# A kernel's transform stage: half of one product moves from VectorE to ScalarE and GpSimd

## The chip, the cores and the metric

One core of a Trainium2 chip runs the whole program. The metric is the device time of one execution in microseconds; the kernel before has a median of 1918.08 us over three runs. The engines are PE (TensorE, matrix products), DVE (VectorE), ACT (ScalarE), POOL (GpSimd) and SP (SyncE, which here only issues DMAs). Each engine works through its own queue in order.

## The reference

Two independent parts are computed and put side by side. Part A is a recurrent attention over 64 segments of 32 rows. Part B, which the change touches, is a long convolution done in the frequency domain:

```python
P = jnp.exp(logdA[:, :, None] * l[None, None, :])
K = jnp.einsum('dn,dnl,dn->dl', Cc, P, dB).real
...
Yf = Uf * Kf[None, :, :, :]
y = irfft2(Yf, s=(1, L2), axes=(-2, -1)).astype(jnp.bfloat16)[:, :, 0, :L]
y = (lambda x, *d: x.transpose(*d))(y, 0, 2, 1) + u * Dskip[None, None, :]
```

Here `u` is 2048 x 1024 in bfloat16, `Uf` and `Kf` are the spectra of `u` and of the convolution's kernel, and their complex product is what the stage below computes.

## The kernel before

The program runs part B first and part A after it; the weights that A keeps on the chip are loaded while B works. Part B builds its tables for some 400 us and writes the spectrum of `u` to DRAM (`Ud`). Then comes the stage of this case, the loop `for b in range(16)` (L1542), where `b` stands for a pair of 256 channels (`b // 4`) and a quarter of the frequencies (`b % 4`).

For every `b` there are two classes of frequencies, 0 and 1. For each class PE computes the kernel's spectrum into PSUM (`spectrum`, L1221, 20 matmuls, tile `pa`, two banks: one for each half `h` of the frequencies, each with a real and an imaginary part of 256 channels). The spectrum of `u` for a class is one 512 KB load into `uq[class]` (`load_u`, L1214, tile `wq`). There is one `uq` for each class, so the load for b+1 waits until block b has read it.

DVE then does the complex product, all in float32:

- `times_u` (L1384) makes two products of 1024 elements for a class: Z, the imaginary part of `u` times the kernel's spectrum, into the SBUF tile `Zs` (tile `z`), and X, the real part times it, in place in PSUM. I call them Z0, X0 for class 0 and Z1, X1 for class 1.
- `rotate` (L1389) joins X and Z in two instructions of 512 elements. For class 0 it writes the tile `even` (`y`); this is the first rotation. For class 1 it works in place in PSUM; this is the second rotation.
- sum and difference of the two classes follow (L1483 into `odd`, L1484 into `even`), two instructions of 1024 elements.

POOL then makes four additions of 512 elements for block b (L1486 twice, L1488, L1489), which leave the product's spectrum in bfloat16 tiles (`Bt`). I call them the additions of b. After them POOL multiplies a tile of `u` with `Dskip` (`skips`, L1503). The inverse transform of block b-4 runs on PE beside this, in two parts (`inverses`, 16 matmuls each and one with the identity, L1537), and ACT brings each part out of PSUM (L1538).

The generator `pointwise` (L1461) holds DVE's part and stops once in its middle: before the stop Z0, X0, the first rotation (for b > 3 after the next two), Z1, X1; behind it the second rotation, `odd`, `even` and POOL's additions. The loop body runs the first half, issues spectrum and inverse for PE, and then runs the second half. For b < 3 the second half is run between the two spectra; for b of 3 and more behind both. `now` holds the PSUM tiles for the next block. Three such tiles are used in turn, so the class 1 spectrum of b+1 goes into the tile that class 0 of block b leaves, which is free once the first rotation of b has read it.

Program order decides who waits for whom: an instruction that reads a place waits for the last one ahead of it in the program that wrote it, whatever the engines. `Zs` has one place for each class.

Of the kernel before, what the change touches and what calls it, by code (L numbers as in the profile page):

```python
# [14 lines left out]
ALU = mybir.AluOpType  # L15
# [697 lines left out]
def part_b(ctx, tc, u, A_re, A_im, B_re, B_im, C_re, C_im, log_dt, Dskip, out_b, ahead, copies, residents, first_state):  # L713
# [5 lines left out]
    DH, DQ = 512, 256  # L719
    v, sc, gp, pe, sy = nc.vector, nc.scalar, nc.gpsimd, nc.tensor, nc.sync  # L720
# [57 lines left out]
    with tc.tile_pool(name="b_par", bufs=1) as par, tc.tile_pool(name="b_parh", bufs=2) as parh, \  # L778
# [127 lines left out]
        parts = {}  # L906
# [62 lines left out]
        for word_ in PAR:  # L969
            word = word_.rstrip("/")  # L970
            nm, n_ = word[0], word[1:]
# [234 lines left out]
    def weighted(kc, n_, amp):  # L1206
        a_ = amp.rearrange("p (j q) -> p j q", j=3)[:, :, 256 * n_:256 * n_ + 256]
        g_ = G[kc][:, n_, 2:5].rearrange("p j s h f -> p j s (h f)")
        v.tensor_tensor(out=g_, in0=g_, in1=a_.unsqueeze(2).to_broadcast([128, 3, 2, 256]), op=ALU.mult)
# [4 lines left out]
    def load_u(b, ns=(0, 1), eng=sy):  # L1214
        for n_ in ns:
            eng.dma_start(out=uq[n_], in_=Ud[b % 4, b // 4][:, 2 * n_:2 * n_ + 2].rearrange("p a c d -> p (a c d)"))

    def load_inverse(i):
        sy.dma_start(out=MI[i][:], in_=MId[2 * i:2 * i + 2].rearrange("c p a k q -> p c a k q"))

    def spectrum(b, n_, outs, woven=()):  # L1221
        dq, kc = b // 4, b % 4
        KT = ks[dq // 2]
        d = slice(DQ * (dq % 2), DQ * (dq % 2) + DQ)
        for i in range(20):
            half, cs, j = i // 10, i // 5 % 2, i % 5
            pe.matmul(outs[half][:, cs, :], lhsT=G[kc][:, n_, j, cs, half, :], rhs=KT[j][:, d], start=(j == 0), stop=(j == 4), skip_group_check=True)
            for k in woven[i * len(woven) // 20:(i + 1) * len(woven) // 20]:
                make(k, 1)
# [100 lines left out]
    for f in range(16):  # L1330
# [7 lines left out]
        if f == 15:  # L1338
# [7 lines left out]
            uq = [t_[:].bitcast(F32) for t_ in wsl[1:3]]  # L1346
# [29 lines left out]
    def make(kc, n):  # L1376
        for _ in range(n):
            next(made[kc])

    def halves(pool=ps_e):  # L1380
        t_ = pool.tile([128, 2, 512], F32, name="pa", tag="pa")
        return [t_[:].rearrange("p h (c d) -> p h c d", c=2)]

    def times_u(s_, Z, n_, X=None):  # L1384
        us = uq[n_].rearrange("p (a c d) -> p a c d", a=2, c=2)
        for i, t_ in ((1, Z), (0, s_[n_][0] if X is None else X)):
            v.tensor_tensor(out=t_, in0=us[:, :, i, :].unsqueeze(2).to_broadcast([128, 2, 2, DQ]), in1=s_[n_][0], op=ALU.mult)  # L1387

    def rotate(Y, X, Z):  # L1389
        v.tensor_tensor(out=Y[:, :, 0, :], in0=X[:, :, 0, :], in1=Z[:, :, 1, :], op=ALU.subtract)  # L1390
        v.tensor_tensor(out=Y[:, :, 1, :], in0=X[:, :, 1, :], in1=Z[:, :, 0, :], op=ALU.add)
    now = [halves() for _ in range(2)]
# [56 lines left out]
    Zs, even = (pw.tile([128, *dims], F32, name=nm) for nm, dims in (("z", (2, 2, 2, DQ)), ("y", (2, 2, DQ))))  # L1449

    def blocks(t_):
        return t_.rearrange("p i c d -> p (i c) d")
# [4 lines left out]
    def spectra(dq, kc, odd_):  # L1457
        at = PLACES[dq].split()[2 * kc + odd_]
        return Bp[:, stay_.index(at)] if at in stay_ else Bq[:, ("e2", "o1", "o3", "s2").index(at)]

    def pointwise(b, s_):  # L1461
        dq, kc = b // 4, b % 4
        if b:
            times_u(s_, Zs[:, 0], 0)
            if b < 4:
                rotate(even, s_[0][0], Zs[:, 0])
                if b < 3:
                    weighted(b + 1, 0, amps[b + 1])
                load_u(b + 1, (0,))
                for i in {1: (0,), 2: (4,), 3: ()}[b]:  # L1470
                    load_inverse(i)
                if b == 1:
                    next(resident)
            times_u(s_, Zs[:, 1], 1)
            if b < 15:
                load_u(b + 1, (1,) if b < 4 else (0, 1))
            if b > 3:
                rotate(even, s_[0][0], Zs[:, 0])
        yield
        if b:  # L1480
            rotate(s_[1][0], s_[1][0], Zs[:, 1])
        Y = (even[:], s_[1][0]) if b else (first[:, 0], first[:, 1])
        v.tensor_tensor(out=odd[:], in0=Y[0], in1=Y[1], op=ALU.subtract)  # L1483
        v.tensor_tensor(out=even[:], in0=Y[0], in1=Y[1], op=ALU.add)  # L1484
        for i, op in ((0, ALU.add), (1, ALU.subtract)):
            gp.tensor_tensor(out=spectra(dq, kc, 0)[:, i], in0=even[:, 0], in1=even[:, 1], op=op)  # L1486
        eng, to = v if b == 15 else gp, blocks(spectra(dq, kc, 1))
        eng.tensor_tensor(out=to[:, 0:4:3], in0=odd[:, 0], in1=odd[:, 1, ::-1], op=ALU.add)  # L1488
        eng.tensor_tensor(out=to[:, 2:0:-1], in0=odd[:, 0], in1=odd[:, 1, ::-1], op=ALU.subtract)  # L1489
# [3 lines left out]
    def rows_of(t_, n_):  # L1493
        return t_[CLASSES[n_ % 4]][:, :, DQ * (n_ // 4):DQ * (n_ // 4) + DQ]

    def load_pair(n_, pool, bufs=4):
        uu = held[n_] = pool.tile([128, 2, 2, DQ], BF16, name="uu", tag="uu", bufs=bufs)
        sy.dma_start(out=uu[:].rearrange("p i a d -> p (i a) d"), in_=rows_of(u_v, n_))
# [6 lines left out]
    def inverses(n_, i):  # L1505
        while ended:
            ended.pop(0)()
        inverse(n_ // 4, PAIRS[2 * n_ % 8 + i], held[n_][:, i])
        if i:
            ended.append(lambda: sc.dma_start(out=rows_of(out_v, n_), in_=held[n_][:].rearrange("p i a d -> p (i a) d")))  # L1510
# [30 lines left out]
    w4 = k1[0:4, 3072:4096]  # L1541
    for b in range(16):  # L1542
        points = pointwise(b, now)
        next(points)
        for _ in range(4 if b in (2, 3) else 0):
            second.pop(0)()
        if b == 2:
            ks.append([])
        if 2 <= b < 6:
            lo, hi = b - 2, min(b - 1, 3) if b < 5 else 5  # L1550
            ks[1].extend(load_k(1, k1[:, DH * lo:DH * hi], lo))
        if b >= 4:
            load_pair(b - 2, iv)
        if b == 3:
            v.tensor_scalar(out=ident[:], in0=ident[:], scalar1=float(PLEN / 2), scalar2=None, op0=ALU.mult)
            load_pair(0, iv)
            load_pair(1, iv)
            state = first_state(g0[0:8, 5120:6144], iv.tile([128, 8, 24], BF16, name="xt0", bufs=1))
            next(state)
            ctx_k.close()  # L1560
            ps_h = ctx.enter_context(tc.tile_pool(name="b_psh", bufs=1, space=PSUM))
            ps_y = ctx.enter_context(tc.tile_pool(name="b_psy", bufs=2, space=PSUM))
        if b == 0:
            now = nxt_
        elif b + 1 < 16:
            now = []
            for n_ in range(2):
                if b < 3 and n_:
                    next(points, None)
                    weighted(b + 1, 1, amps[b + 1])  # L1570
                now.append(halves(ps_h if b > 2 and (2 * b + n_) % 3 == 0 else ps_e))
                spectrum(b + 1, n_, [now[n_][0][:, half] for half in range(2)], (3,) * 7 if b == 1 else ())
                if b >= 4:
                    inverses(b - 4, n_)
        next(points, None)
        for n_ in (0, 1) if b == 3 else (b - 2,) if 3 < b < 15 else ():
            skips(n_, gp)
        for i in {1: (1,), 3: (5,), 4: (2, 3), 5: (6, 7)}.get(b, ()):
            load_inverse(i)
        if b == 2:  # L1580
            rows4 = g0[0:4, 5120:6144]
            for half in range(2):
                sy.dma_start(out=rows4[:, DH * half:DH * half + DH], in_=Kx[half][31, NF - 1].rearrange("g c -> (g c)").partition_broadcast(4))
            sy.dma_start(out=w4, in_=u[0:4, :])
            gp.tensor_tensor(out=w4, in0=rows4[:, 0:D], in1=w4, op=ALU.mult)
            gp.memset(l4, 0.0)
            gp.memset(l4[:, :, 127:128], float(PLEN / 2))
            gp.affine_select(out=l4[:, :, 127:128], in_=l4[:, :, 127:128], compare_op=ALU.is_ge, fill=0.0, base=0, pattern=[[1, 4], [0, 1]],
                             channel_multiplier=-1)
        for _ in range({1: 2, 2: 2, 3: 1, 4: 1, 5: 1, 6: 2, 7: 2, 8: 2, 9: 2, 11: 3, 12: 3, 13: 2, 14: 3, 15: 3}.get(b, 0)):  # L1590
            next(resident)
        if b == 10:
            state.send(ps_y.tile([128, 8, 128], BF16, name="yp", tag="yp")[:, :, 0:8])
# [180 lines left out]
```

## Time and profile before

| what | value |
|---|---|
| times of three runs | 1917.59, 1918.08, 1934.71 us |
| profiled execution | 1915.11 us, span of its instructions 1913.4 us |
| transform loop, about 403 to 560 us | 157 us |
| of it blocks 5 to 14, one after the other | 9.65 us for each |
| end of the last inverse, begin of part A | about 577 us |
| part A, from about 592 us on | 1321 us, DMA share 0.93 |

Rows of the timeline give start, length, engine, line, operation, output and input, shape and count; a bracket at the end tells how long the engine had been idle before it and what ended that. Rows of the windows table give, for a stretch of time, its length, then the busy time of PE, PEld (weight loads), DVE, ACT and POOL, the granted TensorE clock (1.00 is full speed), the share of the DMA engines and GB/s. Rows of the chain of waits give start, length and what the chain ran through.

### The profile page before, as it was taken

How to read it: one execution, taken by the hardware profiler on the slowest of the kernel's cores; microseconds unless marked ns; L12 is line 12 of the kernel's file. 1: busy time of each engine (PE TensorE's matmuls, PEld its weight loads, DVE VectorE, ACT ScalarE, POOL GpSimd, SP SyncE). 2: the span in 40 equal slices, each digit the busy share in tenths (PEclk: the TensorE clock that was granted, in tenths of full speed). 3: DMA queues.
4: the chain of work that ended last, by engine and by line, in shares of the span. 5: the costliest groups of instructions: out<-in, count | busy, mean ns of one | idle time of the engine just before them, and what ended most of it. 6: DMA issues, size and time to landing. Idle time of an engine off the chain costs nothing.

```text
span 1913.4 us, 73735 instructions
## 1 busy us (share of the span) xinstructions
PE 1768.3 (92%) x31563; PEld 1088.4 (57%) x31563; DVE 1349.7 (71%) x3367; ACT 921.2 (48%) x1655; POOL 514.4 (27%) x900
## 2 busy tenths in 40 slices
PE   8999999868986989999999999999999999999989
PEld 3666665546773555555555555555555555555554
DVE  8599999899973666666666666766666666666650
ACT  8799999860112434444343444444343444444420
POOL 2354544427770111111111111111111111212120
PEclk9999999898998999999999999999999999999999
DMA  7889898778799999999999999999999999999993
GB/s 220 238 236 266 258 276 249 219 220 293 258 306 357 348 322 342 341 345 337 344 353 344 338 350 351 336 355 343 340 348 354 330 345 346 346 340 347 352 335 95
DMA packets 341744, 594.21 MB, mean 311 GB/s; under 512 B 94100, under 2 KB 216476, under 8 KB 339368
## 3 DMA queue, kind: packets, MB, share of 16 engines
q1 hardware_dynamic: 297944, 534.99, 81.8%
q10 hardware_dynamic: 36816, 29.59, 4.8%
q0 software_dynamic: 6656, 24.92, 3.5%
q8 instruction: 247, 4.05, 0.8%
q14 instruction: 81, 0.66, 0.1%
HBM read 531.92 MB, written 71.63 MB: 315 GB/s over the span
## 4 chain that ended last, share of the span: by engine, by line
PE 46%; DMA 31%; DVE 12%; ACT 5%; issue 3%; POOL 2%; SPq 1%; DVEq 0%; POOLq 0%; ACTq 0%
PE acc L414 22%; DMA wst<-WD_v 11%; DMA wst<-WD_o 9%; PE pp L527 9%; DMA wst<-WD_q 3%; PE pe L667 3%; DMA wst<-WD_k 2%; PE tr L425 2%; PE pro L184 2%; DVE nr L1274 1%; PE pro L197 1%; DMA arena<-PKd 1%; PE pv L495 1%; DMA wq<-Ud 1%; DVE pa L1387 1%
## 5 line engine op out<-in xcount | busy, mean ns | idle before, releaser
L414 PEld LDWEIGHTS <-a_hT 128*32 128x32 bf16 x12351 | 329.6, 96 | 327.3 <-issue 76.1
L420 ACT CAST arena<-acc 128x512 bf16<-128x512 f32 x384 | 225.2, 586 | 395.1 <-PE acc L414 326.8
L414 PE MATMUL acc<-wst,a_hT 128*32 128x512 bf16 x2308 | 230.1, 382 | 35.3 <-DMA wst<-WD_v 26.1
L527 PEld LDWEIGHTS <-arena 128*32 128x32 bf16 x8256 | 215.4, 96 | 76.9 <-issue 53.6
L428 POOL COPY arena<-arena 128x128 bf16<-128x128 bf16 x128 | 37.6, 294 | 697.6 <-PE tr L425 364.9
L335 DVE TENSOR_SCALAR arena<-keep 128x256 int32<-128x256 int32 x508 | 174.3, 395 | 27.9 <-PE acc L414 27.9
L414 PE MATMUL acc<-XM,a_hT 128*32 128x512 bf16 x2560 | 184.2, 380 | 0.0
L414 PE MATMUL acc<-W,a_hT 128*32 128x512 bf16 x1536 | 132.8, 384 | 0.0
L197 PE MATMUL pro<-XM,wsl 128*128 128x512 bf16 x512 | 124.6, 387 | 2.6 <-DVE kst L206 1.5
L454 DVE TENSOR_REDUCE a_mx<-sc 128x4 f32<-128x160 f32 (+1 forms) x192 | 71.8, 374 | 74.2 <-PE sc L442 72.9
L527 PE MATMUL pp<-W_o,arena 128*32 128x256 bf16 x3584 | 121.7, 273 | 2.3 <-issue 2.2
L544 DVE COPY arena<-tr 128x512 bf16<-128x512 bf16 x64 | 27.2, 425 | 126.3 <-PE tr L425 126.3
L458 ACT ACTIVATE sc<-sc 128x160 f32<-128x160 f32 (+1 forms) x192 | 63.9, 333 | 106.5 <-DVE sc L455 106.0
L462 DVE TENSOR_REDUCE a_mx<-sc 128x4 f32<-128x160 f32 (+1 forms) x192 | 72.7, 379 | 55.2 <-ACT sc L458 54.9
L489 POOL TENSOR_TENSOR arena<-arena,a_BD 128x128 bf16<-128x128 bf16 x128 | 51.3, 401 | 211.5 <-DVE arena L472 201.3
L414 PE MATMUL acc<-W_q,a_hT 128*32 128x512 bf16 x1536 | 107.9, 379 | 0.0
L1274 DVE TENSOR_SCALAR nr<-ptt 128x456 f32<-128x456 int16 x128 | 80.3, 628 | 31.3 <-PE ptt L1252 28.3
L1266 ACT ACTIVATE E<-pa 128x648 bf16<-128x648 f32 x128 | 87.7, 712 | 16.9 <-PE pa L1258 15.2
L623 ACT CAST arena<-pp 128x128 bf16<-128x128 f32 x64 | 17.0, 266 | 154.8 <-DVE arena L623 154.8
L527 PE MATMUL pp<-wst,arena 128*32 128x256 bf16 x1536 | 76.4, 274 | 16.4 <-DMA wst<-WD_o 15.0
L513 ACT CAST arena<-pv 128x512 bf16<-128x512 f32 (+1 forms) x128 | 61.4, 479 | 59.6 <-PE pv L499 33.4
L425 PEld LDWEIGHTS <-arena 128*128 128x128 bf16 x1024 | 57.6, 98 | 54.8 <-issue 25.9
(334 smaller groups left out, 3967.7 us busy)
## 6 DMA issues: line engine op xcount, KB each, us to landing
wst<-WD_v SPq DMA_DIRECT2D x256, 512.0 KB
wst<-WD_k SPq DMA_DIRECT2D x192, 512.0 KB
wst<-WD_o SPq DMA_DIRECT2D x192, 512.0 KB
wst<-WD_q SPq DMA_DIRECT2D x128, 512.0 KB
Ud<-ux POOLq DMA_DIRECT2D x16, 1024.0 KB, 7.5
wq<-Ud SPq DMA_DIRECT2D x32, 512.0 KB
wsl<-in_A_Wk_dram SPq DMA_DIRECT2D x16, 512.0 KB
wsl<-in_A_Wv_dram SPq DMA_DIRECT2D x16, 512.0 KB
```

Of the source, the lines that this page charges most:

```text
L197: nc.tensor.matmul(a[:], lhsT=w[:, kc, 128 * j:128 * j + 128], rhs=xTl[:, kc, :, :].rearrange("p s k -> p (s k)"), start=(kc == 0), stop=( ...
L335: nc.vector.tensor_scalar(out=out.bitcast(I32), in0=in_.bitcast(I32), scalar1=0, scalar2=None, op0=ALU.bitwise_or)
L414: nc.tensor.matmul(a[32 * g:32 * g + 32, o_:o_ + rhs.shape[1]], lhsT=hT[:, kc, :], rhs=rhs, start=(kc == 0), stop=(kc == KC - 1), tile_pos ...
L420: nc.scalar.copy(out=q, in_=a[:])
L425: nc.tensor.transpose(out=p[:, hl, :, :].rearrange("p a b -> p (a b)"), in_=q[:, 128 * hl:128 * hl + 128], identity=ident[:])
L454: nc.vector.tensor_reduce(out=m_, in_=x, axis=AX.X, op=ALU.max)
L458: nc.scalar.activation(out=flat(sc, i), in_=flat(sc, i), func=ACT.Exp, scale=scale)
L462: nc.vector.tensor_reduce(out=m_, in_=x, axis=AX.X, op=ALU.add)
L513: copy(out=o[:, i:i + n], in_=p[:, i:i + n, :].rearrange("p a (g q) -> p a g q", g=4))
L527: nc.tensor.matmul(po[32 * qt:32 * qt + 32, o_:o_ + rhs.shape[1]], lhsT=oT[:, h % 4, (h % 16) // 4, :], rhs=rhs, start=False, stop=(h == 3 ...
L1266: sc.activation(out=T["E", r, e // 4][:, lo:lo + 8 * NE].rearrange("p (i c) -> p i c", i=2), in_=T.pop(("p", r, e))[:, :, 0:4 * NE], func= ...
L1274: v.tensor_scalar(out=T["n", r, e // 4][:, lo:lo + 8 * NT], in0=T.pop(("t", r, e))[:, 0:8 * NT].bitcast(I16)[:, 0:16 * NT:2], scalar1=floa ...
```

## The change

For class 1 DVE's Z1 now covers only the first half of the frequencies (512 elements instead of 1024). For the second half, ACT copies the kernel's spectrum from PSUM into the place in `Zs` (`moved`), and POOL multiplies it there with the imaginary part of `u` (`shared`). The rest of the product is as it was.

```diff
-    def times_u(s_, Z, n_, X=None):
+    def times_u(s_, Z, n_, X=None, parts=2):
         us = uq[n_].rearrange("p (a c d) -> p a c d", a=2, c=2)
-        for i, t_ in ((1, Z), (0, s_[n_][0] if X is None else X)):
-            v.tensor_tensor(out=t_, in0=us[:, :, i, :]..., in1=s_[n_][0], op=ALU.mult)
+        for i, m, t_ in ((1, parts, Z), (0, 2, s_[n_][0] if X is None else X)):
+            v.tensor_tensor(out=t_[:, 0:m], in0=us[:, 0:m, i, :]..., in1=s_[n_][0][:, 0:m], op=ALU.mult)
+    def moved(s_):
+        sc.copy(out=Zs[:, 1, 1], in_=s_[1][0][:, 1])
+    def shared():
+        us = uq[1].rearrange("p (a c d) -> p a c d", a=2, c=2)
+        gp.tensor_tensor(out=Zs[:, 1, 1], in0=us[:, 1, 1, :]..., in1=Zs[:, 1, 1], op=ALU.mult)
...
             times_u(s_, Zs[:, 0], 0)
+            if b > 3 and b < 15:
+                load_u(b + 1, (0,))
...
-            times_u(s_, Zs[:, 1], 1)
+            times_u(s_, Zs[:, 1], 1, parts=1)
             if b < 15:
-                load_u(b + 1, (1,) if b < 4 else (0, 1))
+                load_u(b + 1, (1,))
...
         if b == 0:
             now = nxt_
+            moved(now)
+            shared()
         elif b + 1 < 16:
...
                 spectrum(b + 1, n_, ...)
+                if n_ and b + 1 >= 1:
+                    moved(now)
                 if b >= 4:
                     inverses(b - 4, n_)
+        if b > 2 and b < 15:
+            shared()
         next(points, None)
+        if 0 < b < 3 and b + 1 >= 1:
+            shared()
```

The copy for block b+1 is issued behind the class 1 spectrum of b+1, in the body of block b. The POOL product for b+1 comes after the second half of `pointwise` of b for b = 1 and 2, and ahead of it for b = 0 and for b from 3 to 14. The two loads of `uq` for b+1 were issued together behind X1 for b > 3; now the first stands behind X0.

More of the change, by code (lines that the diff above doesn't have):

```diff
@@ L1382, in halves @@
         return [t_[:].rearrange("p h (c d) -> p h c d", c=2)]
-    def times_u(s_, Z, n_, X=None):
+    def times_u(s_, Z, n_, X=None, parts=2):
         us = uq[n_].rearrange("p (a c d) -> p a c d", a=2, c=2)
-        for i, t_ in ((1, Z), (0, s_[n_][0] if X is None else X)):
-            v.tensor_tensor(out=t_, in0=us[:, :, i, :].unsqueeze(2).to_broadcast([128, 2, 2, DQ]), in1=s_[n_][0], op=ALU.mult)
+        for i, m, t_ in ((1, parts, Z), (0, 2, s_[n_][0] if X is None else X)):
+            v.tensor_tensor(out=t_[:, 0:m], in0=us[:, 0:m, i, :].unsqueeze(2).to_broadcast([128, m, 2, DQ]), in1=s_[n_][0][:, 0:m], op=ALU.mult)
+    def moved(s_):
+        sc.copy(out=Zs[:, 1, 1], in_=s_[1][0][:, 1])
+    def shared():
+        us = uq[1].rearrange("p (a c d) -> p a c d", a=2, c=2)
+        gp.tensor_tensor(out=Zs[:, 1, 1], in0=us[:, 1, 1, :].unsqueeze(1).to_broadcast([128, 2, DQ]), in1=Zs[:, 1, 1], op=ALU.mult)
     def rotate(Y, X, Z):
```

## The prediction

> **What bounds the kernel now.** I read the page first, then the windows table over the transform loop, then the timeline of one block, and the chain of waits for the loads of u.
>
> ```profile
> PE 1768.3 (92%) x31563; PEld 1088.4 (57%) x31563; DVE 1349.7 (71%) x3367; ACT 921.2 (48%) x1655; POOL 514.4 (27%) x900
> ```
>
> ```profile
> 453.00:560.00 107.00, 99.28 (x850) 81.64 (x849) 104.83 (x112) 13.85 (x24) 77.69 (x57) 0.99 0.90 296
> ```
>
> Over the whole span PE is the busiest. In the blocks from b = 5 on it is DVE, with 104.83 of 107 us; ACT has 93 us free there and POOL 29. One block, b = 8, shows how they hang together:
>
> ```profile
> 481.08 1.22 DVE L1484 TENSOR_TENSOR y<-y,pa 128x1024 f32<-128x1024 f32 x1
> 482.22 1.22 DVE L1387 TENSOR_TENSOR z<-wq,pa 128x1024 f32<-128x1024 f32 x1
> ...
> 482.38 2.50 POOL L1486 TENSOR_TENSOR Bt<-y 128x512 bf16<-128x512 f32 x2 [2.53 <-DVE y L1484]
> ...
> 482.89 2.35 PE L1227 MATMUL pa<-k,XM 128*128 128x256 bf16 x20
> ...
> 483.35 1.22 DVE L1387 TENSOR_TENSOR pa<-wq,pa 128x1024 f32<-128x1024 f32 x1
> ...
> 484.48 1.22 DVE L1387 TENSOR_TENSOR z<-wq,pa 128x1024 f32<-128x1024 f32 x1
> 484.60 2.59 SPq L1216 DMA_DIRECT2D wq<-Ud  x2
> ...
> 485.08 1.91 PE L1525 MATMUL yp<-Bt,MI 128*128 128x256 bf16 x16
> 485.62 1.22 DVE L1387 TENSOR_TENSOR pa<-wq,pa 128x1024 f32<-128x1024 f32 x1
> ...
> 486.75 0.68 DVE L1390 TENSOR_TENSOR y<-pa,z 128x512 f32<-128x512 f32 x1
> 486.82 0.38 PE L1537 MATMUL yp<-uu,b_ident 128*128 128x512 bf16 x1
> ...
> 487.29 0.60 ACT L1538 ACTIVATE uu<-yp 128x512 bf16<-128x512 f32 x1 [3.60 <-PE yp L1537]
> 487.30 2.13 POOL L1503 TENSOR_TENSOR uu<-uu,Dsk 128x1024 bf16<-128x1024 bf16 x1
> 487.35 0.68 DVE L1391 TENSOR_TENSOR y<-pa,z 128x512 f32<-128x512 f32 x1
> ...
> 487.94 0.69 DVE L1390 TENSOR_TENSOR pa<-pa,z 128x512 f32<-128x512 f32 x1
> ...
> 488.08 2.34 PE L1227 MATMUL pa<-k,XM 128*128 128x256 bf16 x20 [0.88 <-DVE y L1391]
> ...
> 490.73 1.22 DVE L1484 TENSOR_TENSOR y<-y,pa 128x1024 f32<-128x1024 f32 x1
> ...
> 491.87 1.21 DVE L1387 TENSOR_TENSOR z<-wq,pa 128x1024 f32<-128x1024 f32 x1
> ```
>
> The block lasts from Z0 to the next Z0: 491.87 - 482.22 = 9.65 us, and DVE has no gap in it. The class 1 spectrum of b+1 starts at 488.08, 0.05 us after the first rotation of b ends (487.35 + 0.68): PE waits for DVE. In the program the second rotation (487.94) needs nothing but DVE's own work.
>
> **What the change takes away.** Z1 loses half. Instructions of 1024 elements follow each other at 1.13 us (484.48, 485.62), those of 512 at 0.60 (486.75, 487.35), so DVE saves 0.53 us in each block, 15 blocks, 8 us if nothing else came of it.
>
> **What it moves without effect.** The two loads of u look as if the first had waited behind X1. But the pair begins at 484.60, just as X0 ends (483.35 + 1.22 = 484.57), and ends at 487.19, with X1's end at 486.84 between: SP held each one until its own product had read the tile. To issue the first behind X0 in the program changes nothing: 0 us. The uu load and the weight loads behind it on SP keep their places.
>
> **What it adds.** The copy is 512 float32 from PSUM on ACT; the nearest row is L1538 at 0.60 us with the same input. The POOL product has two float32 inputs and a float32 output of 512; the row with that shape:
>
> ```profile
> L1016 POOL TENSOR_TENSOR ux<-us x16: 1263/1266/1269, 83.6 to 372.3; 128x512 f32<-128x512 f32 x16
> ```
>
> So 1.27 us. POOL's work for a block, from 482.38 to 489.43 (487.30 + 2.13), becomes some 8.3 us. By length alone both fit beside DVE. What decides is their place. From b = 3 on, copy and product of block b+1 write the one place in `Zs` ahead of the second rotation of block b, which reads it. So the second rotation of b takes what b+1's product left there (this changes which product enters that half), and it must wait for this chain: first rotation of b on DVE, class 1 spectrum of b+1 on PE, copy on ACT, product on POOL. Before, none of that stood ahead of the rotation. Behind the waiting rotation DVE has queued `odd`, `even` and the next Z0; POOL's additions of b and PE's next class 0 spectrum wait for those. POOL waits in `shared` with only the additions of b behind it, which could not start anyway, and ACT waits in `moved` with the activation of an inverse that PE does later. So nothing covers the chain: DVE idles through it.
>
> **The new block, b = 5 to 14**, in us from Z0. X1 starts at 2.26 + 0.60 = 2.86 and ends at 4.08; the first rotation takes 4.00 to 5.28. PE starts 0.05 later and takes 2.34: 7.67. ACT starts 0.09 behind PE (486.82 + 0.38 to 487.29) and takes 0.60: 8.36. The product also needs class 1 of u for b+1, loaded behind X1. The chain of waits shows such a load, and a worse one at b = 4:
>
> ```profile
> 486.86 4.57 DMA wq<-Ud
> ```
>
> ```profile
> 445.04 8.15 DMA wq<-Ud
> ```
>
> From X1's end at 4.08 this gives 8.67 at the usual 4.57. So the product starts at about 8.72, ends at 9.99, and the second rotation starts at 10.02. From it to the next Z0 are 491.87 - 487.94 = 3.93 us: 13.95. That is 4.30 more per block, with PE at full clock.
>
> PE now stands idle from the end of the second inverse (7.67 + 2.3 = 10.0) to 13.95 + 0.13, four us in every block. What such a gap does is in the trace at b = 4:
>
> ```profile
> 449.85 0.38 PE L1537 MATMUL yp<-uu,b_ident 128*128 128x512 bf16 x1 [3.01 <-POOL uu L1503]
> ...
> 450.07 3.49 PE L1227 MATMUL pa<-XM 128*128 128x256 bf16 x20
> ```
>
> ```profile
> 450.00:452.00 2.00, 2.00 (x15) 1.56 (x14) 1.97 (x2) 0.60 (x1) 1.89 (x1) 0.77 0.94 362
> 452.00:454.00 2.00, 2.00 (x12) 1.34 (x11) 1.05 (x2) 0.00 (x0) 1.60 (x2) 0.50 1.10 284
> 454.00:456.00 2.00, 2.00 (x16) 1.44 (x15) 2.00 (x3) 0.00 (x0) 2.00 (x2) 0.88 1.07 347
> ```
>
> After a gap of 3.01 us the granted clock fell to 0.50 and the lost time is 2 x (0.23 + 0.50 + 0.12) = 1.7 us. If every block's gap does that, PE's first spectrum and inverse end at 0.13 + 2.19 + 1.91 + 0.38 + 1.7 = 6.3 instead of 4.6, so the class 1 spectrum starts at 6.3, ends at 8.64, the copy ends at 9.33, the product at 10.65, and the block lasts 10.68 + 3.93 = 14.6: 4.96 more. [...] I take 4.96, the row's side, for all ten blocks: 49.6 us.
>
> **The other blocks.** At b = 0 copy and product stand ahead of POOL's additions:
>
> ```profile
> 408.56 0.69 DVE L1390 TENSOR_TENSOR y<-pa,z 128x512 f32<-128x512 f32 x1 [0.74 <-POOL Bt L1486]
> ```
>
> ```profile
> 406.03 2.50 POOL L1486 TENSOR_TENSOR Bt<-y 128x512 bf16<-128x512 f32 x2 [26.86 <-PE pa L1227]
> ```
>
> ```profile
> 406.66 2.72 ACT L1178 ACTIVATE XM<-gf 128x512 bf16<-128x512 int16 x5
> ```
>
> The first rotation of b = 1 overwrites `even` and already waits for two of these additions. ACT is in its own series until 409.38, so the copy ends at 409.98, the product at 411.3, the two additions at 413.8 instead of 408.53: +5.3. In b = 1 and 2 the product stands behind the additions and DVE is busy long enough: only the saving, -1.1.
>
> ```profile
> 435.68 5.39 PE L1227 MATMUL pa<-XM,g 128*128 128x256 bf16 x40
> ```
>
> ```profile
> 437.06 1.22 DVE L1387 TENSOR_TENSOR pa<-wq,pa 128x1024 f32<-128x1024 f32 x1
> ...
> 438.68 0.69 DVE L1390 TENSOR_TENSOR pa<-pa,z 128x512 f32<-128x512 f32 x1
> ...
> 441.46 1.22 DVE L1484 TENSOR_TENSOR y<-y,pa 128x1024 f32<-128x1024 f32 x1
> 442.60 1.21 DVE L1387 TENSOR_TENSOR z<-wq,pa 128x1024 f32<-128x1024 f32 x1
> ...
> 453.28 1.22 DVE L1387 TENSOR_TENSOR z<-wq,pa 128x1024 f32<-128x1024 f32 x1 [0.95 <-DMA wq<-Ud]
> ```
>
> At b = 3 the spectrum ends at 441.07 and the copy at 441.76; X1, half a us earlier, ends at 437.77, so u lands at 442.34. The product runs to 443.66 and the second rotation starts at 443.69 instead of 438.68: +5.0. At b = 4 PE's class 1 spectrum stands behind an inverse that waits for POOL's `skips` (the 3.01 us above) and ends at 453.56, which is 10.88 behind the end of `even` (442.68). Copy, product and the rest make 10.88 + 0.69 + 0.05 + 1.27 + 0.03 + 3.93 + 0.08 = 16.93 from Z0 to Z0 instead of 453.28 - 442.60 = 10.68: +6.25; the 0.95 us wait for u goes. At b = 15 nothing is ahead of the rotation: -0.5.
>
> **Behind the loop** weights and part A follow. A delay could be hidden there only if transfers were behind at its end:
>
> ```profile
> 560.00:562.00 2.00, 0.76 (x5) 0.48 (x5) 2.00 (x3) 0.00 (x0) 2.00 (x2) 1.00 0.18 56
> ```
>
> A DMA share of 0.18 says that they were not, so I let the whole delay through.
>
> **Sum**: 5.3 - 1.1 + 5.0 + 6.25 + 49.6 - 0.5 = 64.5. The profiled execution took 1915.1, so 1979.6; the median, 1918.1, lies 3 us above it: 1982.6, told as 1982.
>
> **Rivals.** [...] Second, u lands late in every block, as the 8.15 at b = 4: the product starts at 12.3, the block is 17.5, 7.9 more each, 94 in all and 2012. Against it: blocks get longer while their transfers stay the same. Third, on the other side: the second rotation finds its operand ready and does not wait. Copy and product then run beside DVE, each block saves 0.53 and only the wait at b = 0 is left: -8 + 5.3 = -2.7, 1915, no change that can be told. It decides if copy and product of b+1 end before the first rotation of b does, 5.28; but the spectrum that they need starts only then. Fourth, the change does nothing it says, with the tail eating the delay: half of the 64.5 hidden gives 1950. Against it is the 0.18.
>
> **Chances.** Forecast 0.56, full clock 0.26, late u 0.06, no wait 0.06, half hidden 0.04, a gain through something not seen 0.02. The range takes the first two with errors of 1 us a block (the price of copy, product and load are from neighbours): 1976 - 10 to 1982 + 20, 1966 to 2002. A change under 1% (19 us) can't be told from none. Slower 0.92, same 0.06, faster 0.02.
>
> **What would show it.** In the profile after: DVE idle ahead of the second rotation (L1390, `pa`), ended by POOL, 12 times with 3 to 6 us; blocks of 14 to 15 us from Z0 to Z0; Z1 at 0.68; the first load of u still starting as X0 ends; granted clock below 1 in the loop if the gaps count. [...]

## The result and the profile after

The changed kernel takes 1986.05 us (median of six runs, 1983.08 to 1989.36), the kernel before 1917.84 us (median of six): 68 us more by the medians. The ratio of the runs is 1.0328, with a 95% interval of 1.0306 to 1.0350, which is 63 us: slower either way. The profiled execution took 1989.36 us, with a span of 1987.6 us.

The page's line of busy times, to set beside the one from before:

```profile
PE 1788.8 (90%) x31563; PEld 1097.7 (55%) x31563; DVE 1344.5 (68%) x3367; ACT 928.6 (47%) x1670; POOL 532.7 (27%) x915
```

DVE has 5 us less to do, ACT 7 and POOL 18 us more, in 15 new instructions each. PE has the same 31563 matmuls and is busy 20 us longer. None of these sums is anywhere near 63 or 68 us: no engine has become the bound by its work. The windows table from 460 to 620 us, which holds blocks 5 to 14 (stretch, length, busy time of PE, PEld, DVE, ACT, POOL, then granted clock, DMA share, GB/s) tells it better:

```profile
460.00:620.00 160.00, 116.52 (x825) 88.72 (x823) 98.74 (x108) 19.69 (x34) 87.62 (x65) 0.85 0.58 189
```

Before, DVE was busy in 104.83 of 107 us; now in 98.74 of 160. Every engine idles, the transfers too (share 0.58 instead of 0.90), and PE's clock is 0.85 instead of 0.99. That is the picture of a chain of waits. The view of the rotation's line says where it ends (total idle time of DVE ahead of this line by what ended it, and how often):

```profile
  POOL z L1394: 68.9, 12
  POOL Bt L1495: 5.9, 1
```

Twelve times, for b = 3 to 14, DVE waits for POOL's product, 68.9 us in all; once, at b = 1, for POOL's additions. Two blocks one after the other show the two forms that the chain takes. First the block b = 8, with Z0 at 510.93 (rows picked from the timeline of all engines):

```profile
510.93 1.21 DVE L1387 TENSOR_TENSOR z<-wq,pa 128x1024 f32<-128x1024 f32 x1
511.07 4.43 PE L1227 MATMUL pa<-k,XM 128*128 128x256 bf16 x20 [4.55 <-DVE y L1493]
512.06 1.22 DVE L1387 TENSOR_TENSOR pa<-wq,pa 128x1024 f32<-128x1024 f32 x1
513.19 0.68 DVE L1387 TENSOR_TENSOR z<-wq,pa 128x512 f32<-128x512 f32 x1
513.31 2.57 SPq L1216 DMA_DIRECT2D wq<-Ud  x2
513.91 1.23 DVE L1387 TENSOR_TENSOR pa<-wq,pa 128x1024 f32<-128x1024 f32 x1
515.29 2.70 PE L1534 MATMUL yp<-Bt,MI 128*128 128x256 bf16 x16
515.65 0.68 DVE L1398 TENSOR_TENSOR y<-pa,z 128x512 f32<-128x512 f32 x1
518.04 2.35 PE L1227 MATMUL pa<-k,XM 128*128 128x256 bf16 x20
520.47 0.58 ACT L1390 COPY z<-pa 128x512 f32<-128x512 f32 x1 [1.57 <-PE pa L1227]
521.13 1.27 POOL L1394 TENSOR_TENSOR z<-wq,z 128x512 f32<-128x512 f32 x1 [3.01 <-ACT z L1390]
522.43 0.70 DVE L1397 TENSOR_TENSOR pa<-pa,z 128x512 f32<-128x512 f32 x1 [6.10 <-POOL z L1394]
```

The first rotation ends at 516.33 (515.65 + 0.68). Then DVE does nothing for 6.10 us, while spectrum, copy and product follow one another. PE's first spectrum took 4.43 us instead of 2.35 and its inverse 2.70 instead of 1.91, after a gap of 4.55 us (granted clock 0.50 from 511 to 515 us), so the class 1 spectrum started only at 518.04, 1.71 us behind the rotation that it waits for. Here PE at the lowered clock is last, and POOL's wait ends with ACT. The next block, picked in the same way:

```profile
526.29 1.21 DVE L1387 TENSOR_TENSOR z<-wq,pa 128x1024 f32<-128x1024 f32 x1
526.43 3.78 PE L1227 MATMUL pa<-k,XM 128*128 128x256 bf16 x20 [3.77 <-DVE y L1493]
529.27 1.23 DVE L1387 TENSOR_TENSOR pa<-wq,pa 128x1024 f32<-128x1024 f32 x1
534.67 0.58 ACT L1390 COPY z<-pa 128x512 f32<-128x512 f32 x1 [1.63 <-PE pa L1227]
536.35 1.26 POOL L1394 TENSOR_TENSOR z<-wq,z 128x512 f32<-128x512 f32 x1 [2.79 <-DMA wq<-Ud]
537.64 0.70 DVE L1397 TENSOR_TENSOR pa<-pa,z 128x512 f32<-128x512 f32 x1 [5.95 <-POOL z L1394]
```

Here PE lost less, the copy was ready at 535.25, and POOL waited another 1.1 us for u: it landed 5.8 us behind X1's end (529.27 + 1.23 = 530.50). Both blocks take 15.2 to 15.4 us. Over all fifteen products POOL's waits divide between the two:

```profile
  ACT z L1390: 41.3, 5
  DMA wq<-Ud: 19.1, 8
```

Of the 41.3 us, 30.9 are one wait at the start of the loop, ahead of the product for b = 1. In blocks 5 to 14 the wait ends with ACT in three (8, 10 and 13) and with the load of u in seven.

### The profile page after: what moved, and what is told of

It is laid out like the page before. It is cut to its first block, busy times and chain, and to the rows that moved or that the text cites. A ratio compares the mean times of both kernels' runs of the same rounds, so it can differ in the third digit from the quotient of the medians.

```text
span 1987.6 us, 73775 instructions
## 1 busy us (share of the span) xinstructions
PE 1788.8 (90%) x31563; PEld 1097.7 (55%) x31563; DVE 1344.5 (68%) x3367; ACT 928.6 (47%) x1670; POOL 532.7 (27%) x915
## 4 chain that ended last, share of the span: by engine, by line
PE 43%; DMA 34%; DVE 13%; ACT 5%; issue 3%; POOL 2%; SPq 1%; POOLq 0%; DVEq 0%; ACTq 0%
PE acc L414 20%; DMA wst<-WD_v 11%; DMA wst<-WD_o 10%; PE pp L527 7%; DMA wst<-WD_k 3%; DMA wst<-WD_q 3%; PE pe L667 3%; DMA wq<-Ud 2%; PE tr L425 2%; PE pro L184 2%; PE pa L1227 2%; DMA arena<-PKd 1%; DVE nr L1274 1%; DVE pa L1387 1%; PE yp L1534 1%
## 5 line engine op out<-in xcount | busy, mean ns | idle before, releaser
L462 DVE TENSOR_REDUCE a_mx<-sc 128x4 f32<-128x160 f32 (+1 forms) x192 | 72.6, 378 | 55.1 <-ACT sc L458 55.0
L1227 PEld LDWEIGHTS <-XM 128*128 128x128 bf16 x480 | 54.3, 115 | 76.4 <-issue 45.4
```

Source lines behind the costliest of these rows:

```text
L462: nc.vector.tensor_reduce(out=m_, in_=x, axis=AX.X, op=ALU.add)
```

## The experiments

Each run's own profile gives the distance from Z0 of b = 1 to Z0 of b = 15 ("loop") and the mean of blocks 5 to 14. These are sharper than the whole time: from Z0 of b = 15 to the end of the span the profiles of these runs took between 1360.0 and 1373.9 us, with no order by what was changed, so single whole times scatter by several us.

| kernel | ratio to before (95%) | median, us | loop, us | blocks 5 to 14, us |
|---|---|---|---|---|
| before | 1 | 1917.84 | 144.28 | 9.65 |
| changed | 1.0328 (1.0306 to 1.0350) | 1986.05 | 213.41 | 15.15 |
| rotate_first | 1.0038 (1.0016 to 1.0060) | 1927.79 | 149.07 | 9.62 |
| b0_order | 1.0331 (1.0283 to 1.0380) | 1985.62 | 205.73 | 14.92 |
| pe_filled | 1.0332 (1.0299 to 1.0366) | 1986.28 | 210.03 | 14.78 |
| u_early | 1.0296 (1.0257 to 1.0336) | 1980.59 | 205.05 | 14.34 |
| filled_and_u | 1.0311 (1.0272 to 1.0350) | 1978.77 | 198.98 | 13.71 |
| best_order | 1.0003 (0.9979 to 1.0027) | 1919.86 | 140.71 | 9.33 |
| half_left_out | 0.9986 (0.9962 to 1.0010) | 1916.45 | 141.18 | 9.57 |
| split_alone | one run | 1916.52 | 143.18 | 9.64 |

The kernel before, beside the experiments, had medians of 1922.34 us (first four) and 1920.56 us (the rest); the ratios are against its runs in the same series.

**rotate_first: is it the order round one place, or the work?**

```diff
             if b > 3:
                 rotate(even, s_[0][0], Zs[:, 0])
+            if b > 2:
+                rotate(s_[1][0], s_[1][0], Zs[:, 1])
         yield
-        if b:
+        if 0 < b < 3:
             rotate(s_[1][0], s_[1][0], Zs[:, 1])
```

> The changed kernel with one move: from b = 3 on the second rotation of block b stands in the first half, right behind the first rotation, so ahead of the copy and the product for b+1 (it then takes its own block's product). Copy and product stay, and stay as long. If the wait comes from the one place in Zs, DVE no longer idles ahead of the second rotation, blocks 5 to 14 take 9.65 - 0.53 = 9.1 us, only the wait at b = 0 (5.3 us) is left, and the time is 1918 + 5.3 - 7.5 = 1916 (1912 to 1922). If the cost lies in the work itself (ACT and POOL now too full, PSUM or SBUF shared by more engines), the blocks stay above 13 us and the time above 1960.

PE, ACT, POOL and SP run the same instructions in the same order as in the changed kernel, and DVE too but for one small instruction at b = 3. Only the place of the rotation in the program, and so whose product it waits for, is another. No rotation waits for POOL's product any more; the view of its line has one entry left, for the additions ahead of the first rotation:

```profile
  POOL Bt L1497: 9.9, 7
```

The loop falls from 213.41 to 149.07 us. So 64 of the 69 us that the loop had lost went with that wait, and copy and product cost next to nothing by their length. The theory of too much work falls: it wanted blocks above 13 us.

The mean block is 9.62, though, not the 9.1 expected, and the time is 1927.79 us, 1.0038 of the kernel before, where 1916 (1912 to 1922) had been expected; 4.5 of the 11.8 us between them are the kernel before, which was itself slower in this series. The timeline of DVE and that of POOL show what came next, at b = 5 (the 2.45 us ahead of its Z0 is a late load of u):

```profile
459.58 1.22 DVE L1387 TENSOR_TENSOR z<-wq,pa 128x1024 f32<-128x1024 f32 x1 [2.45 <-DMA wq<-Ud]
464.93 0.69 DVE L1397 TENSOR_TENSOR y<-pa,z 128x512 f32<-128x512 f32 x1 [1.13 <-POOL Bt L1497]
```

```profile
461.17 1.27 POOL L1394 TENSOR_TENSOR z<-wq,z 128x512 f32<-128x512 f32 x1 [3.12 <-DMA wq<-Ud]
462.40 2.49 POOL L1497 TENSOR_TENSOR Bt<-y 128x512 bf16<-128x512 f32 x2
```

POOL holds the product until u has landed, and the additions that read `even` stand behind it; the next first rotation overwrites `even` and waits for them. It is the same wait as at b = 1, now in six more blocks, 0.3 to 1.1 us each. The blocks without it take 9.24.

**b0_order: the wait at b = 1**

```diff
         if b == 0:
             now = nxt_
             moved(now)
-            shared()
...
-        if 0 < b < 3 and b + 1 >= 1:
+        if b < 3:
             shared()
```

> The changed kernel with the POOL product for b = 1 behind the additions of b = 0, as it already is for b = 1 and 2. If the first rotation of b = 1 waits because these additions come late, the 5.85 us of idle DVE ahead of it go to about 0.7 and the time falls by 5 us, to 1981 (1979 to 1983). If something else is late there (the tables' build, the load of u), the block stays at 18.1 us and the time at 1986.

Block 1 went from 18.12 to 13.00 us, so 5.1 us: the wait was POOL's order. In the changed kernel the timelines of POOL and DVE show it whole, and the last row is the same rotation in b0_order:

```profile
407.26 1.26 POOL L1394 TENSOR_TENSOR z<-wq,z 128x512 f32<-128x512 f32 x1 [30.88 <-ACT z L1390]
408.49 2.47 POOL L1495 TENSOR_TENSOR Bt<-y 128x512 bf16<-128x512 f32 x2
```

```profile
410.99 0.69 DVE L1397 TENSOR_TENSOR y<-pa,z 128x512 f32<-128x512 f32 x1 [5.85 <-POOL Bt L1495]
```

```profile
411.44 0.69 DVE L1397 TENSOR_TENSOR y<-pa,z 128x512 f32<-128x512 f32 x1 [0.73 <-POOL Bt L1495]
```

The whole time does not resolve it: 1985.62 us where 1981 had been expected, but the interval of the ratio spans some 19 us (0.0097 x 1922). The loop does. It fell by 7.7 us in all; of the 2.6 beyond block 1, 2.3 are in blocks 5 to 14, which this edit doesn't touch. So the mean of these blocks moves by some 0.2 us from one profile to the next with nothing changed in them.

**pe_filled, u_early, filled_and_u: what is last inside the chain?** Once by a second class 0 spectrum in PE's gap, once by a product with the class 0 spectrum of u, once by both.

```diff
# pe_filled
+            if b >= 4:
+                spectrum(b + 1, 0, [now[0][0][:, half] for half in range(2)])
         if b > 2 and b < 15:
             shared()
# u_early
     def shared():
-        us = uq[1].rearrange("p (a c d) -> p a c d", a=2, c=2)
+        us = uq[0].rearrange("p (a c d) -> p a c d", a=2, c=2)
```

> The changed kernel with PE's gap filled: from b = 4 on the class 0 spectrum of b+1 is computed a second time behind the inverse, into the same tile with the same result (20 matmuls, 2.35 us at full clock). If the lowered clock after the gap is part of the price, the granted clock in the loop goes from 0.85 to near 1, the class 1 spectrum starts right behind the first rotation, and blocks 5 to 14 go from 15.15 to about 14.0 us: 1974 (1970 to 1978). If the clock costs nothing because the load of u ends later anyway, the time stays at 1986 with the clock near 1.

> The changed kernel with POOL's product taking the class 0 spectrum of u, which lands some 2 us earlier than that of class 1 (so that half of the product is another one). If the load of class 1 is what ends last in most blocks (8 of 15 waits of POOL's product end with that load), blocks 5 to 14 lose 0.5 to 1.5 us: 1972 to 1981. If PE at the lowered clock is last, the two are equal within 0.3 us a block and the time stays above 1982.

> The changed kernel with both at once: PE's gap filled by the repeated class 0 spectrum, and POOL's product taking the class 0 spectrum of u. Alone the first changed little (blocks 5 to 14 at 14.78 instead of 15.15 us) since the load was then last, the second gave 14.34 with PE's lowered clock last. If these two end side by side and the rest is the bare chain, the blocks take 4.08 + 1.28 + 2.39 + 0.69 + 1.32 + 3.96 = 13.6 to 13.7 us, as worked out with full clock, and the time is some 15 us below the changed kernel's (1968 to 1975). If a third thing is hidden in the chain, the blocks stay above 14.0.

Filling the gap brought most of the clock back. The windows table from 465 to 545 us, first the changed kernel, then the filled one:

```profile
465.00:545.00 80.00, 56.57 (x391) 43.13 (x390) 48.75 (x54) 8.90 (x15) 44.65 (x33) 0.82 0.54 175
```

```profile
465.00:545.00 80.00, 61.42 (x511) 50.17 (x514) 51.87 (x57) 8.96 (x16) 45.93 (x34) 0.98 0.56 183
```

From 465 to 615 us, all ten blocks, the granted clock was 0.95 (0.84 in the changed kernel): the gap that was left still lowered it at times, as ahead of a class 0 spectrum at 569.72 us that took 4.00 us. The blocks only went from 15.15 to 14.78, not to 14.0, and the time stayed at 1986.28 us, not 1974: the expectation missed, since u is then last (ten of POOL's thirteen waits end with the load). In the filled kernel's timeline PE starts its class 1 spectrum 0.06 us behind the first rotation (530.30 + 0.68), and POOL still waits:

```profile
530.30 0.68 DVE L1398 TENSOR_TENSOR y<-pa,z 128x512 f32<-128x512 f32 x1
...
531.04 2.36 PE L1227 MATMUL pa<-k,XM 128*128 128x256 bf16 x20 [1.01 <-DVE y L1398]
...
533.48 0.59 ACT L1390 COPY z<-pa 128x512 f32<-128x512 f32 x1 [2.82 <-PE pa L1227]
...
535.31 1.27 POOL L1394 TENSOR_TENSOR z<-wq,z 128x512 f32<-128x512 f32 x1 [2.46 <-DMA wq<-Ud]
```

With u taken early, the waits of POOL's product end with ACT twelve times and with u once, and the blocks fall to 14.34: PE's clock, 0.85 from 465 to 545 us, is then last. With both, the clock there is 1.00 and every block from 5 to 14 takes 13.71 or 13.72 us, as here from Z0 to Z0 in the timeline of DVE:

```profile
483.61 1.21 DVE L1387 TENSOR_TENSOR z<-wq,pa 128x1024 f32<-128x1024 f32 x1
493.46 0.70 DVE L1397 TENSOR_TENSOR pa<-pa,z 128x512 f32<-128x512 f32 x1 [4.46 <-POOL z L1394]
497.32 1.21 DVE L1387 TENSOR_TENSOR z<-wq,pa 128x1024 f32<-128x1024 f32 x1
```

That is the bare chain as expected for it (13.6 to 13.7); nothing third is hidden in it. So of the 5.50 us that a block lost, 4.06 are the chain itself (13.71 - 9.65), and 1.44 are clock and load together: 0.37 and 0.81 when cured alone, more in common, because each covers the other. The 0.37 is not much above the 0.2 by which the mean moves anyway, and its cure was not complete; the other two differences are clear of it.

The whole times do not resolve this: the ratios of the three (1.0332, 1.0296, 1.0311) and that of the changed kernel have intervals that overlap, and filled_and_u ended 4 us above its expected range. Its loop fell by 14.4 us, just what 10 x 1.44 gives.

**best_order and half_left_out: what is the idea worth?** The first moves the rotation and puts POOL's product between the additions that read `even` and those that read `odd` (for b up to 2 behind all four, as in b0_order); the second has no copy and no product, and zeros in that half of `Zs`.

```diff
# best_order, on top of rotate_first
         for i, op in ((0, ALU.add), (1, ALU.subtract)):
             gp.tensor_tensor(out=spectra(dq, kc, 0)[:, i], in0=even[:, 0], in1=even[:, 1], op=op)
+        if b > 2 and b < 15:
+            shared()
         eng, to = v if b == 15 else gp, blocks(spectra(dq, kc, 1))
...
# half_left_out, on the kernel before
-            times_u(s_, Zs[:, 1], 1)
+            times_u(s_, Zs[:, 1], 1, parts=1)
...
```

> The version with the second rotation ahead of copy and product, and POOL's product for b+1 between the two additions that read even and the two that read odd (for b up to 2 behind all four). In the version that only moved the rotation, six first rotations waited for POOL's additions of even, which stood behind a product that waits for u. If that was all that ate the saving, the blocks 5 to 14 take 9.1 us, the loop from b = 1 to 15 takes 144.3 - 7.4 = 137 us and the ratio to the kernel before is 0.996 (0.994 to 0.998). If POOL is too full for a product each block, the blocks stay at 9.6 us and the ratio at 1.00.

> The kernel before with Z1 cut to its first half and nothing in place of the second (that half of Zs holds zeros, so this product is left out): all that the change could gain if copy and product cost nothing. DVE saves 0.53 us in 15 blocks: blocks of 9.1 us, ratio 0.996 (0.994 to 0.998). If DVE's saving is taken up by PE or the loads, blocks stay near 9.6 us and the ratio at 1.00.

Both run at 9.23 to 9.25 us a block wherever u is there in time, so DVE saves 0.41 us a block, not 0.53. In best_order two blocks lose time to u and none from b = 5 on to POOL (timeline of DVE):

```profile
453.77 1.22 DVE L1387 TENSOR_TENSOR z<-wq,pa 128x1024 f32<-128x1024 f32 x1 [2.08 <-DMA wq<-Ud]
473.21 1.22 DVE L1387 TENSOR_TENSOR z<-wq,pa 128x1024 f32<-128x1024 f32 x1 [0.88 <-DMA wq<-Ud]
```

The loop is 3.6 us shorter than before in best_order and 3.1 us in half_left_out, which paid once for a late u, in its DVE timeline:

```profile
474.61 1.22 DVE L1387 TENSOR_TENSOR z<-wq,pa 128x1024 f32<-128x1024 f32 x1 [3.29 <-DMA wq<-Ud]
```

In the whole time neither can be told from the kernel before (1.0003 and 0.9986, both intervals hold 1), short of the 0.996 that was expected for each. So the idea has at most some 6 us in it here (15 x 0.41), and no version beat the kernel before by what can be measured.

**split_alone: the two loads**

```diff
             times_u(s_, Zs[:, 0], 0)
+            if b > 3 and b < 15:
+                load_u(b + 1, (0,))
...
-                load_u(b + 1, (1,) if b < 4 else (0, 1))
+                load_u(b + 1, (1,))
```

> The kernel before with only the loads of u split, the first one behind X0 in the program. If SP held each load until its own product anyway, the first load still starts as X0 ends and blocks 5 to 14 stay at 9.65 us. If the split does start it earlier, b = 5 loses its wait of 0.95 us for u.

At b = 4 X0 and the pair of loads, from the timelines of DVE and SP:

```profile
441.06 1.22 DVE L1387 TENSOR_TENSOR pa<-wq,pa 128x1024 f32<-128x1024 f32 x1
```

```profile
442.31 2.59 SPq L1216 DMA_DIRECT2D wq<-Ud  x2
```

The pair starts at 442.31, 0.03 us behind X0's end, as it did before. The blocks stay at 9.64. The 0.95 us wait at b = 5 is not there in this run, but the load did not start earlier, and the same wait is 0.22 us in half_left_out and 2.08 in best_order: it changes from run to run.

A second place in `Zs`, with the program order left as it is, would have shown the cause in another way; it wasn't tried.

## Why the prediction was right

The forecast was 1982 us from 1966 to 2002, slower with 0.92, through a second rotation that waits for the next block's copy and product. It was 1986, and rotate_first shows that this wait is the cause. That the sum came so near is in part luck: 1.25 us too much at b = 4 stood against 5.5 too little in the ten blocks behind it. Step by step:

- **What the change takes away**: 0.53 us a block was too much; it is 0.41. The short Z1 is followed by X1 after 0.72 us (513.19, 513.91), not the 0.60 read from one short instruction behind another.
- **The loads**: moved without effect, as forecast (513.31 is 0.03 us behind X0's end; split_alone).
- **The copy and the product**: 0.58 and 1.27 us, as read from their neighbours (0.60, 1.27).
- **b = 1**: 18.12 instead of 13.43, 4.7 more; forecast 5.3 less the saving, 4.8. Shown by b0_order. **b = 2**: 0.4 less, forecast 0.5. **b = 3**: 4.8 more, forecast 5.0.
- **b = 4**: 5.0 more, forecast 6.25. The class 1 spectrum took 2.34 us and not the 3.49 of the kernel before: PE's slow time fell on the first spectrum (3.75 us), ahead of the wait for `skips` that covers it.
- **Blocks 5 to 14**: 55.1 us more (151.52 instead of 96.46), forecast 49.6. The chain is right: without a late u and at full clock the forecast's numbers give 13.6, and filled_and_u measured 13.71. The term that was too small is what stands on top, the clock and u. In every block the clock had been taken as last, with 1.7 us lost. A block's clock loss was 1.4 to 2.95 us, and some 2.9 in the three blocks where POOL's wait ends with ACT (4.43 + 2.70 instead of 2.35 + 1.91 in the block shown first). In the other seven u was last: the product started 5.1 to 6.6 us behind X1's end, where the forecast had 4.6 (8.72 - 4.08). So the clock and u were each last, in different blocks: a late u, which the forecast gave 0.06, was true in part, a full clock, with 0.26, in no block. u was the larger miss: with the clock mostly brought back (pe_filled) a block takes 14.78, not 13.95, while with u out of the way (u_early) it takes 14.34, below the 14.6 of the forecast. Why u lands later, though the transfers' share is lower, is not shown.
- **The tail**: the delay went through whole. The loop lost 69.1 us in the profiles, the median 68.2, and from Z0 of b = 15 to the end of the span it took 1371.4 us instead of 1363.7, not less.

After the change all ten gaps ahead of blocks 5 to 14, of 3.48 to 5.78 us, lowered the clock: the class 0 spectrum behind them took 3.64 to 4.43 us, nowhere 2.35. So no run shows the 1976 us, with the clock kept in most of these gaps, from which the range starts at its lower side.

The row with 3.01 us, on which the forecast's choice rested, was one draw. In split_alone the same place has a gap of 3.02 us, and the spectrum behind it ran at full speed:

```profile
447.19 0.38 PE L1539 MATMUL yp<-uu,b_ident 128*128 128x512 bf16 x1 [3.02 <-POOL uu L1505]
447.41 2.34 PE L1227 MATMUL pa<-XM 128*128 128x256 bf16 x20
```

In pe_filled a gap of 2.74 us left the clock as it was, and a shorter one lowered it:

```profile
540.60 2.34 PE L1227 MATMUL pa<-k,XM 128*128 128x256 bf16 x20 [2.74 <-DVE y L1493]
569.72 4.00 PE L1227 MATMUL pa<-k,XM 128*128 128x256 bf16 x20 [2.38 <-DVE y L1493]
```

So in these runs the length of a gap alone does not decide between 2.38 and 3.02 us. The ten gaps of the changed kernel are all longer; the row with 3.01 us could not tell what they would do.

## What to carry to other kernels

When a step of one loop turn is prepared in the turn before, ask first whether the place that it writes still has a reader to come: in this kernel the engine that should have been relieved waited for the whole preparation. From b = 3 on the reader then even takes the next block's product. The saving was 0.4 us a block, the wait 3.5 to 6.7 us. And put work for an idle engine behind whatever frees a tile for the critical engine: length alone said that POOL had room, but its order cost 5 us at one place.

## What was not expected of the hardware

PE's gaps cost more than their length in the changed kernel, through the clock after them: it was 0.85 from 460 to 620 us, and PE was busy 20 us longer in the whole span with the same matmuls. To compute a spectrum twice brought the granted clock from 0.82 to 0.98 between 465 and 545 us at no price that shows.

Some of DVE's products in bfloat16 and some of POOL's work took longer where they overlapped. In the changed kernel's timelines at b = 2:

```profile
424.60 2.03 DVE L1209 TENSOR_TENSOR XM<-XM,wq 128x1536 bf16<-128x1536 bf16 x1
```

```profile
424.55 1.26 POOL L1498 TENSOR_TENSOR Bt<-od 128x512 bf16<-128x512 f32 x1
425.95 1.80 POOL L1394 TENSOR_TENSOR z<-wq,z 128x512 f32<-128x512 f32 x1
```

Of the six DVE products of this form (L1209, `XM`) four took 0.95 us and two 2.02 and 2.03. These two began 0.05 to 0.06 us behind an addition of POOL (424.60 behind 424.55, 412.20 behind 412.14), which kept its usual 1.26 us. POOL's product at 425.95 began while the DVE product had 0.68 us left and took 1.80 us; the other fourteen took 1.26 to 1.27. The kernel before has two such DVE products too: 2.02 and 2.04 us at 409.77 and 422.58, behind additions at 409.72 and 422.52. The float32 products of DVE beside POOL's additions kept their 1.21 to 1.23 us. Why the ones are slowed and the others not is not shown.
